# Converting float64 weights with one ScalarE Prelu and two DVE operations, with the prologue and the first batch's runs in a new order

## Chip, cores and metric

One Trainium2 chip, one of its cores. The metric is the device time of one launch in microseconds; the kernel before takes 1564.34 us, the median of three runs (1562.92 to 1564.81). Engines by the profile's names: PE multiplies matrices, ACT applies functions, DVE and POOL do elementwise work, SP issues every DMA.

## The reference

Eight batches, 8 heads, 576 rows, head dimension 64: first 32 packed queries p attend to k and v, then q attends to the packed result, which serves as keys and as values. The output, 4608 tokens of 512 numbers, passes two MLPs of width 2048:

```
pp  = softmax(p k^T / 8) v;   x = softmax(q pp^T / 8) pp
x   = elu(x @ w_in1) @ w_out1
out = (P(h) / (Q(h) + 1e-6)) @ w_out2,  h = x @ w_in2
P(h) = a0 + a1 h + a2 h^2 + a3 h^3;  Q(h) = 1 + |b0||h| + |b1| h^2
```

The four weight matrices arrive as float64, everything else as float32.

## The kernel before

**Precision and tiling.** Each float32 product of the MLPs runs as three matmuls on a split into hi and lo parts (hi hi, hi lo, lo hi). In the first phase a batch's 576 columns form two halves of 288, and a batch is 32 steps (half n, block f of 128 of the 2048 hidden rows). Step s has `a_h` (L316, 6 matmuls into h), `a_act1` (L325, L326: Exp, then Relu), `a_dve1` (L331: g), `a_hi` (L336, ACT's cast ghi), `a_lo` (L341, DVE's glo) and `a_o` (L351, 12 matmuls into four accumulators acc). A run of steps that add into the accumulators ends with `a_evac`; in the first batch a half takes two runs, and the first run's sum is kept in a tile (xpart) and added at the end. The second phase (from some 770 us) runs the second MLP on blocks of 512 tokens; nothing of it is touched.

**The weights.** w_in is cut into four column blocks c of four pieces (i, c, kt), w_out into 16 pieces (o, f); each piece is 128x512. Since s = A pp and x w_in = A (pp w_in), `m_pe` (L276) multiplies a column block with the batch's packed result once it is there, and `m_hi`, `m_lo` (L286, L290) split it: steps with f in column block c need m of c. A piece is loaded raw (two words a number) and converted by `c0` (scaling of the upper words by 2^-112, on ACT or POOL, and where needed a Sign on ACT), `c1` (bit operations on DVE: L431 AND, L433 shift, L438 shift-OR, L441 OR of the lower words' bits) and `c2` (POOL multiplies by the sign). For w_out `c3` (ACT, L501) and `c4` (POOL, L505) split into hi and lo. `w2_up`, `w2_bits`, `w2_hi`, `w2_lo` do this for the second MLP's 32 pieces, six in a batch, from the second batch on, and spill them to DRAM.

**Order.** All engines' queues are written out by hand, in program order. The prologue does the first batch's attention, the first column block's conversion and warm matmuls without use. Then a loop over s from -2 runs, in this order: loads due (`ldq`), `a_h(s+2)`, PE extras (`peq`), `a_hi(s+1)`, `a_act1(s+2)`, `c1` of the pieces due at s with `a_lo(s+1)` between its parts, `a_dve1(s+2)`, other elementwise work (`ewq`), `a_o(s)`. Tuples give the steps: WO and WI for `c1` of the pieces (`c0` a step earlier, `c3` and `c4` one and two later), MS for m of column blocks 1 to 3, SCH for the next batch's attention. Raw pieces pass through buffers whose own weights come later; a buffer that `c1` sets free is loaded again at once (`loads`, `loaded`, on SP's queue in this order). Before, the buffers of k and v hold four raws as well (`spare_open`).

Of the kernel before, what the change touches and what calls it, by code (L numbers as in the profile page):

```python
# [17 lines left out]
# A float32 product runs as three float32r passes (hi*hi + hi*lo + lo*hi) over  # L18
# exact splits x = hi + lo, hi = x rounded to float32r, lo = x - hi.
# [3 lines left out]
def packed_attention_moe_moe2_kernel(  # L23
    ctx: ExitStack,
    tc: tile.TileContext,
    qT: bass.AP,     # [B, 128=(r d), 4, S]   head = 2 j + r
    kT: bass.AP,     # [B, 128=(r d), 4, S]
    v: bass.AP,      # [B, S, H*D]
    pT: bass.AP,     # [B, 128=(r d), 4, 32]
    w_in1: bass.AP,  # [512, 2048] of 32-bit words, or of pairs of them  # L30
    w_out1: bass.AP, # [2048, 512]
    w_in2: bass.AP,  # [512, 2048]
    w_out2: bass.AP, # [2048, 512]
    a2: bass.AP,     # [128, 4]
    b2: bass.AP,     # [128, 2]
    out: bass.AP,    # [4608, 512]
# [320 lines left out]
    def a_evac(s):  # L357
        # whether a sum is complete
# [34 lines left out]
    # piece: ("i", c, kt) or ("o", f), of the first or the second MLP  # L393
# [25 lines left out]
    def w_e(eng, e, raw):  # L419
        hi = words(raw)[1]  # L420
        if eng is nc.scalar:
            eng.activation(e, hi, AF.Copy, scale=2.0 ** -112)
        else:
            eng.tensor_scalar(e, hi, 2.0 ** -112, 0.0, ALU.mult, ALU.add)

    def w_bits(ws, mid=None):
        # (float32 to fill, scaled upper words, raw, room for the signs if taken)
        ws = [(w.bitcast(U32), e.bitcast(U32), *words(raw), sg) for w, e, raw, sg in ws]
        for w, e, lo, hi, sg in ws:
            if sg is not None:  # L430
                nc.vector.tensor_scalar(sg.bitcast(U32), hi.bitcast(U32), 0x80000000, None, ALU.bitwise_and)  # L431
            else:
                nc.vector.tensor_scalar(e, e, 3, None, ALU.logical_shift_left)  # L433
        if mid:
            mid()
        for w, e, lo, hi, sg in ws:
            if sg is not None:
                nc.vector.scalar_tensor_tensor(  # L438
                    e, e, 3, sg.bitcast(U32), ALU.logical_shift_left, ALU.bitwise_or)
        for w, e, lo, hi, sg in ws:  # L440
# [20 lines left out]
    def c0(p, eng, signed):  # L461
        cw[p] = d = dict(raw=raws.pop((0, p)), e=scr.pop(0))
        if F64:
            w_e(eng, d["e"][1], d["raw"])
            if not signed:
                d["sg"] = scr.pop(0)
                nc.scalar.activation(d["sg"][1], words(d["raw"])[1], AF.Sign)

    def c1(ps, mid=None):
        ys = []  # L470
        for p in ps:
# [6 lines left out]
            ys.append(None if "sg" in d else scr.pop(0))  # L478
        if F64:
            w_bits([(cw[p]["w"], cw[p]["e"][1], cw[p]["raw"], y and y[1]) for p, y in zip(ps, ys)], mid)  # L480
# [5 lines left out]
        for p, y in zip(ps, ys):  # L486
            if y:
                scr_free(y)
# [19 lines left out]
    # the second MLP's: on the way, to DRAM as hi and lo  # L508
    w2t = {}

    def w2_up(piece):
        e = T.tile([128, 512], F32, tag="cvt", name=f"cvt{piece}", bufs=2)
        w2t[piece] = [raws.pop((1, piece)), e]
        if F64:
            w_e(nc.gpsimd, e, w2t[piece][0])

    def w2_bits(piece):
        w = T.tile([128, 512], F32, tag="w", name=f"w{piece}")
        raw, e = w2t[piece]
        if F64:  # L520
            w_bits([(w, e, raw, w)])
# [124 lines left out]
    # =====================================================================  # L646
    with tc.manual_schedule():
# [12 lines left out]
        signed = {p: p[0] == "o" and p[1] not in UNS for p in seq}  # L660
        at_seq = {p: i for i, p in enumerate(seq)}
        slot = {}
        spare = []
        count = [0]

        def loads(n=len(seq)):
            for _ in range(n):
# [8 lines left out]
                elif spare:  # L676
                    slot[i] = (None, spare.pop(0))
                    t = slot[i][1]
# [8 lines left out]
        def spare_open(tag):  # L687
            t = P.tile([128, 2, RW], RDT, tag=tag, name=f"raw_{tag}")
            spare.extend(t[:, i, :] for i in range(2))

# [5 lines left out]
        loads(PL[0])  # L696
# [16 lines left out]
        # keeps the tensor engine's clock up while the first loads arrive  # L713
# [16 lines left out]
        i0, i1 = io[:2]  # L730
        G = nc.gpsimd
# [6 lines left out]
        spare_open("k")  # L738
        loads(EX)
        c0(i0[0], G, False)  # L740
        for r in range(2):
            s1_max(0, r)
            s1_exp(0, r, ("E", "A")[r])
            if r == 0:
                c0(i0[1], G, False)
        c1([i0[0]])
        c2(i0[0])
# [6 lines left out]
        t1_ew(0, 0, engs=(A, A))  # L754
        t1_ew(0, 1, "A", engs=(A, A))
        c1([i0[1]])
        c2(i0[1])
        pp_pe(0, 0, extra("ppx0"))
        pp_pe(0, 1, extra("ppx1"))
        spare_open("v")  # L760
        loads(EX)
        c0(i0[2], A, False)
        c0(i0[3], A, False)
# [4 lines left out]
        warm(WARM[4])  # L768
        c1([i0[2]])
        c2(i0[2])  # L770
        c1([i0[3]])
        c2(i0[3])
        s2_pe(0, 0)
        warm(WARM[5])
        c0(oo[0], A, True)
        s2_max(0, 0)
        s2_sub(0, 0, V)
        m_pe(0, 0, extra("mx"))
        if EARLY:
# [29 lines left out]
        def seq_at(s, a, *fns):  # L809
            # fns a step apart; a pair goes to both queues of its step  # L810
# [18 lines left out]
        def consts():  # L829
            # -a0..-a3, unused, |b1|, Ln bias, Exp bias  # L830
# [189 lines left out]
```

## Time and profile before

| | us |
|---|---|
| median of three runs | 1564.34 |
| span of the profiled execution | 1561.9 |
| busy PE, DVE, ACT, POOL | 1521.0, 1140.2, 1025.3, 424.4 |

The profile gives the profiled execution's span, from the first to the last instruction; no separate time of that execution is given, and the runs lie 1.0 to 2.9 us above the span. A row of the order of time tells start, length, engine, line, operation, out<-in, and in brackets the idle time before it and what ended that. A matmul row's length is modelled. In the windows the clock is the granted share of PE's 2.4 GHz.

### The profile page before, as it was taken

The page shows a single profiled execution, that of the slowest core. Times are in us where ns is not written, and L with a number is a line of the kernel's source. Part 1 is how long each engine was busy: PE and PEld are TensorE (multiplying, and loading weights), DVE is VectorE, ACT ScalarE, POOL GpSimd, SP SyncE. Part 2 cuts the span into 40 slices and gives each one's busy share as a digit, 9 for nine tenths or more (in the row PEclk, how much of TensorE's full clock was granted, in tenths as well). Part 3 has the DMA queues.
Part 4 walks back from the last instruction along what each step waited for, and adds up shares of the span by engine and source line. Part 5 has one row for each costly group of instructions (what it writes and reads, how often), then busy time and mean ns, then how long its engine had stood idle before and what let it go on. Part 6 is the DMA issues. An engine that isn't in the chain of part 4 may idle for free.

```text
span 1561.9 us, 25689 instructions
## 1 busy us (share of the span) xinstructions
PE 1521.0 (97%) x9890; PEld 1314.1 (84%) x9890; DVE 1140.2 (73%) x1857; ACT 1025.3 (66%) x1903; POOL 424.4 (27%) x329
## 2 busy tenths in 40 slices
PE   6799999999999999999999999999999999999999
PEld 5678989889898988999988888888888888888887
DVE  5997686776768677554497777778687777778786
ACT  4576566565656656565586777767677767767675
POOL 3664241322214132210122222222222222222221
PEclk8899999999999999999999999999999999999999
DMA  9343443533344353103930202020010202020000
GB/s 347 128 143 108 159 144 116 174 114 126 119 159 144 115 174 109 65 1 141 381 109 1 82 0 81 1 81 1 19 64 1 81 1 81 1 81 0 28 0 28
DMA packets 64172, 144.80 MB, mean 93 GB/s; under 512 B 4784, under 2 KB 24496, under 8 KB 61232
## 3 DMA queue, kind: packets, MB, share of 16 engines
q1 hardware_dynamic: 64048, 143.15, 25.9%
q8 instruction: 77, 1.26, 0.3%
q14 instruction: 47, 0.39, 0.1%
HBM read 98.04 MB, written 45.09 MB: 92 GB/s over the span
## 4 chain that ended last, share of the span: by engine, by line
PE 83%; DVE 11%; ACT 3%; issue 2%; DMA 1%; SPq 0%; POOL 0%; ACTq 0%; DVEq 0%; POOLq 0%
PE accb L631 25%; PE hb L578 25%; PE acc L351 20%; PE h L316 9%; DVE glo L341 1%; DVE g L331 1%; PE m L276 1%; DVE m L290 1%; DVE s2m L245 1%; DMA raw0('i', 0, 3)_97<-in_w_in_dram 1%; ACT e L326 1%; PE s L129 1%; ACT e L325 1%; PE pp L179 1%; DVE s2m L244 1%
## 5 line engine op out<-in xcount | busy, mean ns | idle before, releaser
L351 PE MATMUL acc<-ghi,wo 128*128 128x288 f32 x2048 | 461.2, 301 | 3.3 <-POOL wo L505 2.7
L578 PE MATMUL hb<-xb,w 128*128 128x512 f32 x1728 | 414.6, 389 | 0.0
L351 PEld LDWEIGHTS acc<-ghi,wo 128*128 128x128 f32 x2048 | 343.4, 189 | 46.2 <-ACT e L325 21.3
L578 PEld LDWEIGHTS hb<-xb,w 128*128 128x128 f32 x1728 | 324.4, 188 | 67.3
L631 PE MATMUL accb<-wo,ghi 128*128 128x512 f32 x1152 | 354.6, 389 | 0.0
L623 POOL TENSOR_TENSOR glo<-g,ghi 128x512 fp32r<-128x512 f32 x143 | 185.6, 1298 | 586.9 <-ACT ghi L621 583.8
L351 PE MATMUL acc<-glo,wo 128*128 128x288 f32 x1024 | 304.7, 298 | 11.3 <-DVE glo L341 11.0
L316 PE MATMUL h<-A,m 128*128 128x288 f32 x1536 | 248.4, 297 | 12.6 <-ACT A L262 3.8
L631 PEld LDWEIGHTS accb<-wo,ghi 128*128 128x128 f32 x1152 | 216.2, 188 | 44.7
L341 DVE TENSOR_TENSOR glo<-g,ghi 128x288 fp32r<-128x288 f32 x256 | 162.0, 633 | 106.7 <-ACT ghi L336 106.1
L316 PEld LDWEIGHTS h<-A,m 128*128 128x128 f32 x1536 | 219.4, 190 | 14.4 <-DVE m L290 4.2
L631 PE MATMUL accb<-wo,glo 128*128 128x512 f32 x576 | 224.1, 389 | 0.0
L336 ACT CAST ghi<-g 128x288 fp32r<-128x288 f32 x256 | 110.6, 432 | 151.4 <-PE acc L351 85.6
L351 PEld LDWEIGHTS acc<-glo,wo 128*128 128x128 f32 x1024 | 193.2, 189 | 15.8 <-DVE glo L341 15.7
L331 DVE SCALAR_TENSOR_TENSOR g<-e,h 128x288 f32<-128x288 f32 x256 | 115.3, 450 | 96.2 <-ACT e L326 95.6
L612 DVE SCALAR_TENSOR_TENSOR Q<-Q,L 128x512 f32<-128x512 f32 x144 | 99.8, 693 | 103.0 <-ACT L L606 103.0
L592 ACT ACTIVATE w<-hb,ab_sb 128x512 f32<-128x512 f32 x144 | 98.5, 684 | 88.5 <-PE hb L578 88.5
L621 ACT CAST ghi<-g 128x512 fp32r<-128x512 f32 x144 | 89.7, 623 | 95.8 <-PE accb L631 61.1
L325 ACT ACTIVATE e<-h 128x288 f32<-128x288 f32 x256 | 105.1, 411 | 63.7 <-PE h L316 62.6
L631 PEld LDWEIGHTS accb<-wo,glo 128*128 128x128 f32 x576 | 108.2, 188 | 22.6 <-DVE glo L623 0.2
L615 DVE SCALAR_TENSOR_TENSOR g<-t,cf,Q 128x512 f32<-128x512 f32 x144 | 108.3, 752 | 16.6 <-DVE Q L613 0.5
L326 ACT ACTIVATE e<-e 128x288 f32<-128x288 f32 x256 | 113.9, 445 | 8.1
(412 smaller groups left out, 1696.8 us busy)
## 6 DMA issues: line engine op xcount, KB each, us to landing
xb<-x2d SPq DMA_DIRECT2D x18, 1024.0 KB, 7.3
x2d<-x SPq DMA_DIRECT2D x30, 576.0 KB, 3.4
out_dram<-o SPq DMA_DIRECT2D x35, 256.0 KB, 2.1
v<-in_v_dram SPq DMA_DIRECT2D x8, 1024.0 KB, 6.3
w<-wi2d SPq DMA_DIRECT2D x8, 1024.0 KB, 10.8
wo<-wo2d SPq DMA_DIRECT2D x16, 512.0 KB, 11.4
k<-in_kT_dram SPq DMA_DIRECT2D x7, 1152.0 KB, 6.5
q<-in_qT_dram SPq DMA_DIRECT2D x7, 1152.0 KB, 5.2
```

What stands on the lines that cost most here:

```text
L316: nc.tensor.matmul(ps[:, :TA], lhsT=m[:, wx, r, c0:c0 + 128], rhs=A[:, ax, r, :], start=(i == 0), stop=(i == 5))
L325: nc.scalar.activation(d["e"], d["h"][:, :TA], AF.Exp)
L326: nc.scalar.activation(d["e"], d["e"], AF.Relu, scale=-1.0, bias=1.0)
L331: nc.vector.scalar_tensor_tensor(d["g"], d["e"], -1.0, d["h"][:, :TA], ALU.mult, ALU.max)
L336: nc.scalar.copy(d["ghi"], d["g"])
L341: nc.vector.tensor_tensor(d["glo"], d["g"], d["ghi"].bitcast(F32), ALU.subtract)
L351: nc.tensor.matmul(acc[m][:, :TA], lhsT=w[:, wx, m * 128:(m + 1) * 128], rhs=d[g], start=(first and i == 0), stop=(last and i == 2))
L578: nc.tensor.matmul(ps, lhsT=w[:, k, c0:c0 + 128], rhs=x[:, k, :], start=(i == 0), stop=(i == 3 * NKD - 1))
L612: nc.vector.scalar_tensor_tensor(Q, Q, 1.0 + 1e-6, r, ALU.add, ALU.mult)
L615: nc.vector.scalar_tensor_tensor(d["g"], t, cf[:, 0:1], Q, ALU.add, ALU.mult)
L623: eng.tensor_tensor(d["glo"], d["g"], d["ghi"].bitcast(F32), ALU.subtract)
L631: nc.tensor.matmul(acc[m], lhsT=d[g][:, m * 128:(m + 1) * 128], rhs=w[:, wx, :], start=(f == 0 and i == 0), stop=(f == NF - 1 and i == 2))
```

## The change

One Prelu on ACT gives a non-negative float for either sign: scale 2^-112 as before, and for negative numbers a slope of -2^32, which adds 32 to the exponent, so that the shift by three moves a bit into the sign's place. Sign, AND, shift-OR and POOL's multiply are gone, in both MLPs. The first batch's runs are four steps of half 0, eight of half 1, twelve of half 0, eight of half 1. Pieces, m and loads have new steps; only the first column block is converted, and o0 scaled, ahead of the loop. Scratch is one pair in wo15 and four tiles; k's and v's buffers hold no raws. The diff, cut:

```diff
-    EARLY = 1
-    S2 = -2
-    MS = (1, 11, 17)
+    RUNS = (0, 0, 4), (1, 0, 8), (0, 4, 16), (1, 8, 16)
+    MS = (5, 13, 17)
-    UNS = (3, 7, 8, 9, 11, 12, 14)
-    EA = (1, 2, 3, 8, 12)
-    WO = (-2, -1, 0, 0, 1, 2, 3, 4, 13, 13, 15, 16, 17, 18, 19, 21)
-    WI = (-2, -2, -1, -1, 5, 6, 8, 7, 10, 11, 11, 12)
+    WO = (-2, -1, 0, 1, 5, 6, 7, 8, 12, 13, 14, 15, 16, 17, 18, 19)
+    WI = (1, 2, 3, 4, 8, 9, 10, 11, 12, 13, 14, 15)
-    NWS = NF - 3
-    PL, EX = (2, 2, 6), 2
+    NWS = NF - 1
...
-            g, i = divmod(t, NF // 2)
-            return b, g % 2, i + NF // 2 * (g // 2), (i == 0, i == NF // 2 - 1)
+            for n, f0, f1 in RUNS:
+                if t < f1 - f0:
+                    return b, n, f0 + t, (t == 0, t == f1 - f0 - 1)
+                t -= f1 - f0
...
+    def w_e(e, raw):
+        nc.scalar.activation(e, words(raw)[1], AF.Prelu, scale=2.0 ** -112, alpha=-2.0 ** 32)
     def w_bits(ws, mid=None):
+        ws = [(w.bitcast(U32), e.bitcast(U32), words(raw)[0]) for w, e, raw in ws]
+        for w, e, lo in ws:
+            nc.vector.tensor_scalar(e, e, 3, None, ALU.logical_shift_left)
         if mid:
             mid()
+        for w, e, lo in ws:
             nc.vector.scalar_tensor_tensor(w, lo, 29, e, ALU.logical_shift_right, ALU.bitwise_or)
...
-    def c2(p):
-        d = cw[p]
-        if "sg" in d:
-            nc.gpsimd.tensor_tensor(d["w"], d["w"], d["sg"][1], ALU.mult)
-            scr_free(d["sg"])
...
         load_k(0, HALVES)
-        loads(PL[0])
+        loads(1)
         load_v(0)
         lq = load_q(0, HALVES)
         next(lq)
-        loads(PL[1])
+        loads(3)
         next(lq)
-        loads(PL[2])
+        loads(1)
         nc.sync.dma_start(out=ab_sb[:, 0:4], in_=a2)
         nc.sync.dma_start(out=ab_sb[:, 4:6], in_=b2)
+        loads()
...
+        t1_ew(0, 0, engs=(A, V))
+        t1_ew(0, 1, "A", engs=(A, V))
+        c0(i0[0])
         pp_pe(0, 0, extra("ppx0"))
         pp_pe(0, 1, extra("ppx1"))
+        c1([i0[0]])
         pp_ew(0, 0)
         pp_ew(0, 1)
         ppt_pe(0, extra("pptx"))
         ppt_ew(0)
         warm(WARM[4])
+        s2_pe(0, 0)
+        c0(i0[1])
+        warm(WARM[5])
+        s2_max(0, 0)
+        c1([i0[1]])
+        c0(i0[2])
+        s2_sub(0, 0, V)
+        s2_exp(0, 0)
         c1([i0[2]])
+        c0(i0[3])
         s2_sum(0, 0)
         s2_mul(0, 0, V)
+        c1([i0[3]])
+        m_pe(0, 0, extra("mx"))
+        s2_pe(0, 1, extra("s2x"))
+        c0(oo[0])
         s2_tr(0, 0)
         s2_hi(0, 0)
+        m_hi(0, 0, slice(0, 256))
+        s2_lo(0, 0, V)
+        m_lo(0, 0, slice(0, 256))
+        s2_max(0, 1, "E")
+        s2_sub(0, 1)
+        m_hi(0, 0, slice(256, 512))
         m_lo(0, 0, slice(256, 512))
+        s2_exp(0, 1)
+        s2_sum(0, 1)
+        warm(WARM[6])
...
-        at(ldq, 13, scr_close, "wo")
-        at(ldq, 14, scr_k)
+        at(ldq, 19, scr_close, "wo")
...
-            seq_at(S2, (0, 1), s2_sum, s2_mul, s2_tr, s2_hi, s2_lo)
+        seq_at(-2, (0, 1), s2_mul, s2_tr, s2_hi, s2_lo)
```

## Rows read from the trace of the kernel before

**Rows 1.** Page, busy us of each engine (share of the span) xinstructions.
```profile
PE 1521.0 (97%) x9890; PEld 1314.1 (84%) x9890; DVE 1140.2 (73%) x1857; ACT 1025.3 (66%) x1903; POOL 424.4 (27%) x329
```

**Rows 2.** Windows: from:to length, busy us by engine (xinstructions), clock, DMA share, GB/s.
```profile
34.00:62.00 28.00, 16.70 (x81) 13.36 (x80) 26.36 (x38) 12.35 (x26) 18.43 (x14) 0.65 0.41 147
62.00:109.00 47.00, 42.51 (x409) 37.32 (x407) 43.06 (x76) 37.90 (x84) 30.47 (x25) 1.00 0.44 155
109.00:140.00 31.00, 28.77 (x257) 23.62 (x250) 27.41 (x50) 19.42 (x41) 19.18 (x15) 1.00 0.18 64
```

**Rows 3.** Timeline of PE, 31 to 63 us: start, us, what, [idle before <-releaser].
```profile
31.82 0.40 PE L316 MATMUL h<-A,m 128*128 128x288 f32 x1 [3.77 <-ACT A L262]
...
41.89 0.61 PE L351 MATMUL acc<-glo,wo 128*128 128x288 f32 x1 [3.00 <-DVE glo L341]
...
62.07 0.30 PE L351 MATMUL acc<-ghi,wo 128*128 128x288 f32 x1
```

**Rows 4.** Chain of waits, first 160 us: start, us, what (one step of PE).
```profile
97.58 0.79 PE h L316 x6
98.38 1.60 PE acc L351 x12
```

**Rows 5.** Timeline of DVE and POOL, 33 to 42 us.
```profile
33.15 0.42 DVE L433 TENSOR_SCALAR scr_cvt<-scr_cvt 128x512 uint32<-128x512 uint32 x1
...
34.20 0.69 DVE L441 SCALAR_TENSOR_TENSOR scr_wo<-raw0('o', 0)_100,scr_wo 128x512 uint32<-128x512 uint32 x1
...
36.02 0.45 DVE L331 SCALAR_TENSOR_TENSOR g<-e,h 128x288 f32<-128x288 f32 x1
...
38.44 1.34 POOL L250 TENSOR_TENSOR s2x<-s2x,s2m 128x576 f32<-128x576 f32 x1
38.69 1.37 DVE L433 TENSOR_SCALAR scr_whi<-scr_whi 128x512 uint32<-128x512 uint32 x1
...
41.38 0.45 DVE L341 TENSOR_TENSOR glo<-g,ghi 128x288 fp32r<-128x288 f32 x1
```

**Rows 6.** DMA issues of the first 60 us: issue, count, KB each, us to landing.
```profile
raw0('i', 0, 3)_97<-in_w_in_dram SPq DMA_DIRECT2D x1, 512.0 KB, 13.6
...
raw0('i', 2, 2)_414<-in_w_in_dram SPq DMA_DIRECT2D x1, 512.0 KB, 3.9
```

**Rows 7.** Timeline of ACT at 20 us.
```profile
20.53 0.68 ACT L422 ACTIVATE scr_wo<-raw0('i', 0, 3)_97 128x512 f32<-128x512 f32 x1 [1.27 <-DMA raw0('i', 0, 3)_97<-in_w_in_dram]
```

**Rows 8.** Groups of ACT, 32 to 104 us: busy us, mean ns | idle before.
```profile
L326 ACT ACTIVATE e<-e 128x288 f32<-128x288 f32 x18 | 8.0, 445 | 0.6
L336 ACT CAST ghi<-g 128x288 fp32r<-128x288 f32 x18 | 7.7, 430 | 12.9 <-DVE g L331 11.0 <-PE acc L351 1.0 <-DVE sm L151 0.9
L325 ACT ACTIVATE e<-h 128x288 f32<-128x288 f32 x18 | 7.4, 410 | 4.1 <-PE h L316 4.0
L501 ACT CAST wo<-scr_wo 128x512 fp32r<-128x512 f32 x6 | 3.6, 604 | 0.0
```

**Rows 9.** Waits, 135 to 770 us: us in total, times, longest us.
```profile
PE acc L351 <- DVE glo L341: 8.0, 12, 1.2
```

**Rows 10.** Timeline, 197 to 214 us (the second batch).
```profile
197.87 0.40 PE L351 MATMUL acc<-glo,wo 128*128 128x288 f32 x1 [0.32 <-DVE glo L341]
...
206.66 0.43 ACT L336 CAST ghi<-g 128x288 fp32r<-128x288 f32 x1 [2.62 <-DVE g L331]
...
210.60 0.69 DVE L438 SCALAR_TENSOR_TENSOR cvt('i', 0, 3)_2445<-cvt('i', 0, 3)_2445,w('i', 0, 3)_2491 128x512 uint32<-128x512 uint32 x1
210.67 1.92 POOL L267 TENSOR_TENSOR A<-s2y,A 128x576 fp32r<-128x576 f32 x1 [2.56 <-ACT A L262]
...
211.33 1.81 DVE L441 SCALAR_TENSOR_TENSOR w('i', 0, 3)_2491<-raw1('i', 0, 3)_2277,cvt('i', 0, 3)_2445 128x512 uint32<-128x512 uint32 x1
...
213.56 0.40 PE L351 MATMUL acc<-glo,wo 128*128 128x288 f32 x1 [1.16 <-DVE glo L341]
```

**Rows 11.** Timeline of ACT at the start.
```profile
0.74 1.28 ACT L648 ACT_TABLE_LOAD   x1 [0.74 <-PEq L1008]
```

More of the change, by code (lines that the diff above doesn't have):

```diff
@@ L412, in words @@
         return two[:, :, 0], two[:, :, 1].bitcast(F32)
[L419 to L424, printed above, removed]
-    def w_bits(ws, mid=None):
[L428 to L433, printed above, removed]
+    def w_e(e, raw):
+        nc.scalar.activation(e, words(raw)[1], AF.Prelu, scale=2.0 ** -112, alpha=-2.0 ** 32)
+    def w_bits(ws, mid=None):
+        ws = [(w.bitcast(U32), e.bitcast(U32), words(raw)[0]) for w, e, raw in ws]
+        for w, e, lo in ws:
+            nc.vector.tensor_scalar(e, e, 3, None, ALU.logical_shift_left)
         if mid:
             mid()
[L436 to L440, printed above, removed]
+        for w, e, lo in ws:
             nc.vector.scalar_tensor_tensor(w, lo, 29, e, ALU.logical_shift_right, ALU.bitwise_or)
@@ L459, in packed_attention_moe_moe2_kernel, with c0 @@
     cw = {}
-    def c0(p, eng, signed):
+    def c0(p):
         cw[p] = d = dict(raw=raws.pop((0, p)), e=scr.pop(0))
         if F64:
[L464 to L467, printed above, removed]
+            w_e(d["e"][1], d["raw"])
     def c1(ps, mid=None):
-        ys = []
         for p in ps:
@@ L477, in c1 @@
                 d["w"] = wi[p[1]][:, p[2], :]
-            ys.append(None if "sg" in d else scr.pop(0))
         if F64:
-            w_bits([(cw[p]["w"], cw[p]["e"][1], cw[p]["raw"], y and y[1]) for p, y in zip(ps, ys)], mid)
+            w_bits([(cw[p]["w"], cw[p]["e"][1], cw[p]["raw"]) for p in ps], mid)
         else:
@@ L485, in c1 @@
                 mid()
-        for p, y in zip(ps, ys):
-            if y:
-                scr_free(y)
+        for p in ps:
             if p[0] == "i":
@@ L514, in w2_up @@
         if F64:
-            w_e(nc.gpsimd, e, w2t[piece][0])
+            w_e(e, w2t[piece][0])
     def w2_bits(piece):
@@ L520, in w2_bits @@
         if F64:
-            w_bits([(w, e, raw, w)])
+            w_bits([(w, e, raw)])
         else:
@@ L659, in packed_attention_moe_moe2_kernel @@
         seq = sorted(when, key=lambda p: when[p])
-        signed = {p: p[0] == "o" and p[1] not in UNS for p in seq}
         at_seq = {p: i for i, p in enumerate(seq)}
         slot = {}
-        spare = []
         count = [0]
@@ L675, in loads @@
                     slot[i] = (fs[0], None)
-                elif spare:
-                    slot[i] = (None, spare.pop(0))
-                    t = slot[i][1]
                 elif used.count("t") < 2:
@@ L685, in loads @@
                 count[0] += 1
-        def spare_open(tag):
-            t = P.tile([128, 2, RW], RDT, tag=tag, name=f"raw_{tag}")
-            spare.extend(t[:, i, :] for i in range(2))
         def loaded(p):
@@ L729, in packed_attention_moe_moe2_kernel @@
             scr_open("wo", [t[:, i, :] for i in range(2)])
-        i0, i1 = io[:2]
-        G = nc.gpsimd
+        i0 = io[0]
         at_new(0)
@@ L737, in packed_attention_moe_moe2_kernel @@
         warm(WARM[1])
-        spare_open("k")
-        loads(EX)
-        c0(i0[0], G, False)
         for r in range(2):
@@ L743, in packed_attention_moe_moe2_kernel @@
             s1_exp(0, r, ("E", "A")[r])
[L744 to L747, printed above, removed]
         t1_pe(0, 0, extra("t1x"))
@@ L753, in packed_attention_moe_moe2_kernel @@
         s1_inv(0, 1)
[L754 to L757, printed above, removed]
+        t1_ew(0, 0, engs=(A, V))
+        t1_ew(0, 1, "A", engs=(A, V))
+        c0(i0[0])
         pp_pe(0, 0, extra("ppx0"))
         pp_pe(0, 1, extra("ppx1"))
[L760 to L763, printed above, removed]
+        c1([i0[0]])
         pp_ew(0, 0)
@@ L837, in packed_attention_moe_moe2_kernel @@
         at(ewq, 24, consts)
-        def scr_k():
-            sk = P.tile([128, 4, 512], F32, tag="k", name="scr_k")
-            scr_open("k", [sk[:, i, :] for i in range(4)])
         for p in seq[NKD:]:
@@ L846, in packed_attention_moe_moe2_kernel @@
             if p not in cw:
-                at(ewq, max(-2, t - 1), c0, p, A if p[0] == "i" or p[1] in EA else G, signed[p])
+                at(ewq, max(-2, t - 1), c0, p)
             cvq.setdefault(t, []).append(p)
-            fns = ([] if signed[p] else [c2]) + ([c3, c4] if p[0] == "o" else [])
-            for k, fn in enumerate(fns):
-                at(ewq, t + 1 + k, fn, p)
-        at(ldq, 13, scr_close, "wo")
-        at(ldq, 14, scr_k)
+            if p[0] == "o":
+                at(ewq, t + 1, c3, p)
+                at(ewq, t + 2, c4, p)
+        at(ldq, 19, scr_close, "wo")
         for c in range(1, NC):
@@ L856, in packed_attention_moe_moe2_kernel @@
                 at(q, MS[c - 1], fn, 0, c)
-        if EARLY:
-            seq_at(S2, (0, 1), s2_sum, s2_mul, s2_tr, s2_hi, s2_lo)
-        else:
-            s2_at(-2, 0, 1)
+        seq_at(-2, (0, 1), s2_mul, s2_tr, s2_hi, s2_lo)
         at(ldq, LK, load_k, 1)
```

25 lines of the change are left out of this document (removed).

## The prediction

> **What bounds the kernel now.** I read the page's busy shares first, then windows over the start, then PE's own order of time there, and only then the engines that feed it. PE is busy 97% of the span [rows 1], so at most 40.9 us (1561.9 - 1521.0) are idle time, plus what PE loses at a lower clock. The windows show where: from 34 to 62 us PE is busy 16.70 of 28 us at a mean granted clock of 0.65, while DVE is busy 26.36; from 62 to 109 PE is busy 42.51 of 47 at full clock, from 109 to 140 it is 28.77 of 31 [rows 2]. So the first steps of the first batch are bound by DVE, the rest of that batch nearly by PE. PE's order of time says the same step by step: the first h starts at 31.82, the second matmul of the first acc step waits 3.00 us for DVE's glo until 41.89, and the fourth acc step starts only at 62.07 [rows 3]; at full clock a step is 0.79 for h and 1.60 for acc, 2.39 us [rows 4]. Between 36.02, when DVE makes the first g, and 62.07 lie 26.05 us for three and a bit steps.
>
> Why DVE is late is in its own rows. A shift takes 0.42 us and an OR 0.69 when alone; a shift that begins while POOL is in a tensor_tensor (38.44 to 39.78) takes 1.37, and the glo that PE waits for comes only at 41.38, behind such shifts [rows 5].
>
> **The conversion.** Before, a weight piece with its sign taken along costs DVE an AND (like the shift, 0.42), a shift-OR (0.69) and an OR (0.69); one without costs DVE shift and OR (1.11), ACT a Sign and POOL a multiply of some 1.3, as its other tensor_tensors [rows 5, 10]. Of the 32 pieces of the first MLP 9 are of the first kind, 23 of the second; half of the upper-word scalings run on POOL. After, every piece is one ACT Prelu, one shift and one OR. DVE saves 9 x 0.69 = 6.2 us. ACT goes from 39 Sign and Copy passes to 32 Prelu passes; I price a Prelu like the Copy on the same strided words, 0.68 [rows 7]. No row shows a Prelu: from below the exp step's 0.41, from above a pass and one table load, 0.68 + 1.28 (rival three). POOL loses 23 multiplies and 16 scalings. What POOL loses matters through DVE: each POOL operation can hold up a DVE one by about its length.
>
> The stretching is told by the Trainium skill too ("SBUF — State Buffer", section "SBUF: two separate sides"): GpSimd and a DVE instruction that needs the shared port pair exclude one another, and the first to start keeps it to its end. The trace agrees: the shift-OR that began 0.07 us ahead of POOL's subtraction took 0.69, the OR behind it 1.81 [rows 10].
>
> **The first three steps.** Between 34 and 62 us DVE now has, at unstretched durations: six conversions (o1, o2, o3, and three of the second column block) x (0.42 + 0.69) = 6.7, four steps of g and glo x 0.90 = 3.6, a last transpose under 1: 11.2 us against 26.36 [rows 2, 5]. POOL still does the low parts of o0 to o2 and two operations of the attention there; five operations that hold DVE up by half a microsecond each make it 13.7. ACT has per step Exp 0.41, Relu 0.45 and the cast 0.43, plus a Prelu and the cast of a wo 0.60 [rows 8]: 2.6 us, 3.9 in the step with two Prelus and the A cast, 12 to 13 us in all. So 13.5 us stand where 26.05 stood: 12.5 saved. Bounds: 16 us at most saved (PE's four steps of 2.39 at full clock [rows 4] stay), 7 if every POOL operation stretches DVE as the 1.37 and 1.81 rows do and ACT's order adds waits.
>
> **The prologue.** SP now issues i0's first piece, v, a half of q, three more pieces, the other half, o0, a and b, then twelve pieces in a row. The bytes ahead of i0's last piece are the same, so it lands when it did, 13.6 us after its issue, where ACT takes it up at 20.53 [rows 6, 7]; v has one piece of 0.5 MB fewer ahead of it, 1 to 2 us (an estimate: ten half megabytes had landed by 20.5), so the pp products can start earlier. The sign multiply (1.3) leaves the chain to m. Against that DVE, in order, now converts three pieces inside the chain max, subtract, exp, sum, multiply (3.3 us, of which 1.1 lie beside the exp), and the first Exp of the MLP stands on ACT behind the second half's s2_exp, which waits for POOL's subtraction. I take 1.5 us earlier for the first g; bounds -2.2 (two conversions in the chain with nothing won) and +4.
>
> **The order of runs.** Four steps of half 0, then eight of half 1, instead of eight and eight: the second column block, which had to be there at step 4, is due at step 8, so its four pieces leave the prologue, and A of half 1 is due at step 4 instead of 8, which the s2 pieces just reach. The same products are formed and the same number of partial sums stored; the store after step 3 costs 4 copies as that after step 7 did. k's and v's buffers no longer hold raw weights, so SP's load of the next k isn't held behind them. The price: with one step between, some late raws are issued when a slot falls free and read by ACT a step later (i3's last at 13 to 14, o15 at 17 to 18). A lone load takes 3.9 us [rows 6], a step 2.4 to 4: ACT may stand 1 to 2 us at each, with its casts queued behind it.
>
> **The rest of the first batch.** From 62 to 109 PE needs 42.5 and one m product more that was earlier before; ACT was busy 37.90 [rows 2], loses some 4 passes of 0.68, gains 4 casts of 0.60 and the m cast, 1.2 as two of them [rows 8]: 38.8. But steps 12 to 15 carry two conversions each, on ACT 1.29 + 1.36 + 0.60 = 3.2 us a step, with the m cast 4.4. At most 4 us can be won; lost, four steps of 0.9 and the m cast, 5: I take 1.0 won here and 0.5 of the 2.2 idle us up to 140.
>
> **Batches two on.** The second MLP's 32 pieces each lose the AND and the shift-OR for a shift, DVE 0.69 less, and the scaling moves from POOL to ACT. PE waits 8.0 us for glo in 12 places there, at most 1.2 [rows 9]: in each of five batches one like the 1.16 of 213.56 [rows 10] and one of 0.32. The long ones stand behind AND, shift-OR and an OR that POOL's subtraction (from 210.67) stretched to 1.81 [rows 10]. With the shift at the AND's place the OR starts near 210.5, ahead of POOL, and glo can start near 211.2, a stretched OR earlier; the short ones need 0.32 of 0.69. ACT's added pass falls in that batch in the 2.62 us in which ACT waits for g [rows 10]. I take 6 us of 7.5; bounds 0 (POOL wins the start) and 7.5. By the skill's rule above the five long waits go if the OR starts first, 5.8 us, and stay if POOL does.
>
> **Sum.** Saved 12.5 + 1.5 + 1.0 + 0.5 + 6.0 = 21.5 us: span 1561.9 - 21.5 = 1540.4. The runs' median, 1564.34, lies 2.4 above this profile's span, so the time is about 1543.
>
> **Rivals.**
> 1. *ACT is the new bound.* Every scaling now sits in ACT's queue ahead of casts that PE needs, and late raws stop it. For it: 38.8 of 47 us and the clumped steps; against: the Signs go. The first steps then save 8 and the stretch to 140 loses 4, with 5 in the later batches: 1564.3 - 9 - 1.5 = about 1554.
> 2. *PE bound from the first step.* The lower clock of 0.65 came with PE's idle stretches [rows 2]; if they go at once, the first steps save 16, the prologue 3, the rest of the batch 5, and later batches 7.5: 1533.
> 3. *The Prelu changes the table.* The trace has one table load in all, 1.28 us at 0.74 [rows 11], and Exp, Relu, Sign and Copy run under it; nothing in it shows Prelu. If Prelu is not in that set, each of 64 needs a load and the next Exp another, 2.57 us: 27 in the first batch's steps where ACT is full, 69 us, and 32 later, each 2.57 less the 1.1 us that ACT is idle in a step (2.39 - 1.29 [rows 4, 8]), 47; less the prologue's and DVE's gain of 21: about 1660. It ends slower than now from the ninth such pair on ACT's critical steps (21.5 / 2.57). The Trainium skill ("ScalarE: Activation LUTs", section "Table sets: the hidden batching unit") says that cheap functions are in every set and names relu, copy, identity and abs, not Prelu; no run here shows it.
> 4. *The second part of the gain doesn't come.* The added ACT pass makes ghi late in later batches as often as DVE's relief makes glo early: 1549.
>
> **Chances.** Forecast 0.58 (its own range 1536 to 1550), rival one 0.15, two 0.10, three 0.06, four 0.11. The 1533 of rival two and the 1554 of rival one set the range: 1533 to 1555. A measurement of this kernel tells about 0.2% (3.1 us) from no change. Faster: all but rival three and the bad end of rival one, 0.89; same 0.03; slower 0.08.
>
> **What would show it.** In the profile after: the first g at 34 to 35, the fourth acc step at 46 to 50 instead of 62.07, DVE's shifts mostly 0.42, POOL far below its 18.43 of 28 us in the first steps; the waits of PE for glo after 140 us down to 1 or 2 us; a Prelu near 0.68 and one table load. Wrong it would be if ACT's cast is what PE waits for in steps 11 to 18, if the first h starts later than 31.82, or if more table loads stand in ACT's rows.

## The result, and the profile after

The changed kernel takes 1545.41 us (median of four runs, 1544.90 to 1547.23), against 1564.55 us for the kernel before (median of four): a ratio of 0.9879, 95% interval 0.9865 to 0.9893. It is 1.2% faster. The forecast was 1543.0 with a range of 1533 to 1555, so size and side were right; the sum behind it was not right in every term, and one half of the change, the new order, turned out to cost time.

The page of the profile after (span 1543.9 us), the line that answers to [rows 1]:

```profile
PE 1516.7 (98%) x9890; PEld 1311.7 (85%) x9890; DVE 1099.6 (71%) x1818; ACT 1038.8 (67%) x1926; POOL 352.9 (23%) x258
```

DVE lost 41 us and POOL 72, ACT gained 13.5; the span lost 18.0. The windows of [rows 2] in the kernel after:

```profile
34.00:62.00 28.00, 25.16 (x175) 22.15 (x176) 24.97 (x46) 21.79 (x48) 8.65 (x7) 0.88 0.54 187
62.00:109.00 47.00, 38.60 (x368) 33.42 (x366) 36.81 (x75) 31.77 (x69) 12.30 (x10) 0.93 0.45 152
109.00:140.00 31.00, 31.00 (x276) 26.64 (x274) 22.82 (x45) 20.30 (x44) 11.69 (x8) 1.00 0.32 114
```

The first window is the gain: PE is busy 25.16 of 28 us in place of 16.70, at a clock of 0.88 in place of 0.65. The second is the surprise: PE is busy 3.9 us less than before there, at a clock of 0.93 in place of 1.00. PE's timeline, the answer to [rows 3] (first h, first glo product, fourth acc step):

```profile
30.58 1.83 PE L316 MATMUL h<-A,m 128*128 128x288 f32 x12
...
37.41 0.44 PE L351 MATMUL acc<-glo,wo 128*128 128x288 f32 x1
...
47.65 0.29 PE L351 MATMUL acc<-ghi,wo 128*128 128x288 f32 x1
```

The wait of 3.00 us for the first glo is gone and the fourth acc step starts 14.4 us earlier. What becomes of that lead is read at a marker that every version has once in five steps, ACT's cast of a second-MLP weight. ACT's timeline before, and then after:

```profile
167.81 0.62 ACT L528 CAST whi('i', 0, 0)_1945<-w('i', 0, 0)_1913 128x512 fp32r<-128x512 f32 x1 [0.45 <-DVE w('i', 0, 0)_1913 L441]
...
638.28 0.60 ACT L528 CAST whi('o', 15)_8128<-w('o', 15)_8096 128x512 fp32r<-128x512 f32 x1
```

```profile
157.80 0.60 ACT L504 CAST whi('i', 0, 0)_1888<-w('i', 0, 0)_1857 128x512 fp32r<-128x512 f32 x1
...
620.21 0.61 ACT L504 CAST whi('o', 15)_8040<-w('o', 15)_8009 128x512 fp32r<-128x512 f32 x1
```

So the lead is 14.4 us at the fourth step, only 10.0 at the first piece of the second MLP (167.81 - 157.80) and 18.1 at the last (638.28 - 620.21). In the kernel before the first of these casts waits 0.45 us for the old conversion of its own piece, which belongs to the later batches; without that the lead there is 9.6. So 4.9 us are lost in the rest of the first batch, and 8.5 are won in the five later ones. Of the 4.9 some 1.1 us are work put off: the kernel before has formed m of column block 1 by its fourth step, the changed one forms it behind its fifth, and at the seventh, where both have it, the lead is 13.3 (71.50 before, 58.19 after).

The largest loss in this stretch is at one place. Three windows, and then the timeline of all engines in the second of them:

```profile
70.00:80.00 10.00, 9.61 (x110) 8.29 (x110) 8.66 (x20) 6.72 (x17) 0.54 (x1) 1.00 0.20 75
80.00:90.00 10.00, 5.41 (x35) 4.47 (x36) 4.91 (x12) 5.00 (x11) 1.47 (x1) 0.66 0.44 152
85.68:89.70 4.02, 4.02 (x18) 3.98 (x19) 1.12 (x5) 0.58 (x1) 0.00 (x0) 0.50 0.28 106
```

```profile
80.77 1.09 PE L274 MATMUL m<-wi,ppT 64*32 64x512 f32 x16 [0.83 <-ACT E L143]
...
83.38 0.98 ACT L284 CAST m<-m 128x1024 fp32r<-128x1024 f32 x1
84.40 1.22 DVE L288 TENSOR_TENSOR m<-m,m 128x1024 fp32r<-128x1024 f32 x1 [1.28 <-ACT m L284]
...
85.68 1.11 PE L157 MATMUL t<-ident,E 128*128 128x128 f32 x4 [3.81 <-DVE sm L149]
...
86.66 0.59 PE L351 MATMUL acc<-ghi,wo 128*128 128x288 f32 x1
...
89.69 1.15 PE L316 MATMUL h<-A,m 128*128 128x288 f32 x6
```

At step 13 PE forms m of column block 2, then has the transposition of the second head half's scores next in its order, and stands 3.81 us. The page names DVE's sm (a 0.14 us operation), but sm stands in DVE's queue right behind the low part of m at 84.40, which is the operation that ended. PE's next h needs m only a step later. But the transposition and m use the same PSUM buffer (the pool "misc" has one), so the transposition waits until m's high part (ACT) and low part (DVE) are read out, and the accumulations of step 13 stand behind it in PE's order. The granted clock averages 1.00 from 70 to 80 us, 0.66 from 80 to 90 and 0.50 from 85.68 to 89.70: after the pause PE runs at the lower of its two levels, 1.2 in place of 2.4 GHz, where the transposition takes 1.11 in place of 0.60 us (e1 below) and the step's accumulations, 86.66 to 89.69, take 3.03 in place of 1.60 [rows 4].

### The profile page after: what moved, and what is told of

Its sections match the earlier page's. It is cut to its first block, busy times and chain, and to the rows that moved or that the text cites. A ratio compares the mean times of both kernels' runs of the same rounds, so it can differ in the third digit from the quotient of the medians.

```text
span 1543.9 us, 25589 instructions
## 1 busy us (share of the span) xinstructions
PE 1516.7 (98%) x9890; PEld 1311.7 (85%) x9890; DVE 1099.6 (71%) x1818; ACT 1038.8 (67%) x1926; POOL 352.9 (23%) x258
## 4 chain that ended last, share of the span: by engine, by line
PE 90%; DVE 5%; ACT 2%; issue 1%; DMA 1%; POOL 0%; SPq 0%; ACTq 0%; POOLq 0%; DVEq 0%
PE accb L607 25%; PE hb L554 25%; PE acc L351 23%; PE h L316 11%; PE m L274 2%; DMA v<-in_v_dram 1%; DVE glo L341 1%; PE s L127 1%; DVE s2m L243 1%; DVE m L288 1%; PE pp L177 1%; ACT e L325 1%; ACT e L326 1%; DVE g L331 0%; PE s L210 0%
## 5 line engine op out<-in xcount | busy, mean ns | idle before, releaser
L591 DVE SCALAR_TENSOR_TENSOR g<-t,cf,Q 128x512 f32<-128x512 f32 x144 | 108.3, 752 | 16.6 <-DVE Q L589 0.5
```

The costliest lines, as they stand in the source:

```text
L591: nc.vector.scalar_tensor_tensor(d["g"], t, cf[:, 0:1], Q, ALU.add, ALU.mult)
```

## The experiments

Two questions: what made the pause at step 13, and which half of the change, the conversion or the new order, won the time. Three chips were used, on which the kernel before takes 1563.61 us (e1, e2, e4, e7), 1564.21 (e5, e6, e8, e10) and 1565.06 (e12 to e15). Each ratio is to the kernel before on the same chip; a difference of medians between chips is known to 1 or 2 us only.

**e1: the transposition one step later.**

```diff
-    SCH = ((6, 8, 10), (12, 13, 15)), (18, 24), (20, 22, 26, 30)
+    SCH = ((6, 8, 10), (12, 14, 15)), (18, 24), (20, 22, 26, 30)
```

> The changed kernel with the scores' transposition of the second head half put at step 14 in place of 13 (SCH's second tuple 12, 14, 15), nothing else. Theory (one PSUM buffer): at step 13 the product m of block 2 and this transposition share the single misc buffer in PSUM; PE issues the transposition and has to wait for m's split on ACT and DVE, 3.8 us, and the accumulations behind it in PE's queue stand as well; the clock falls in the pause. Apart, the wait of 3.81 us in front of the transposition goes, the granted clock between 80 and 90 us stays above 0.9, and the whole gets 4 to 7 us shorter than the changed kernel (about 1540, range 1538.5 to 1541.5). Rival (load of step 13: two conversions, the split of m and the softmax's work are too much for ACT and DVE wherever they are put): the wait moves to the next instruction of PE that needs DVE, and the time stays within 1.5 us of the changed kernel's 1545.4.

Measured 1540.97 us (ratio to before 0.9854, 0.9841 to 0.9868): 4.4 us less than the changed kernel. The window 80 to 90 us in e1, and then the waits around step 14 and the marker:

```profile
80.00:90.00 10.00, 7.84 (x97) 6.21 (x97) 7.12 (x17) 8.03 (x19) 2.78 (x2) 1.00 0.57 200
```

```profile
83.76 0.53 PE L316 MATMUL h<-A,m 128*128 128x288 f32 x2 [0.78 <-ACT m L284]
85.02 0.80 PE L316 MATMUL h<-A,m 128*128 128x288 f32 x4 [0.72 <-DVE sm L149]
85.66 0.60 PE L157 MATMUL t<-ident,E 128*128 128x128 f32 x4
...
152.73 0.60 ACT L504 CAST whi('i', 0, 0)_1888<-w('i', 0, 0)_1857 128x512 fp32r<-128x512 f32 x1
```

The 3.81 us became 0.78 and 0.72, for m itself, which h of step 16 needs, and the clock stays at 1.00. The pause's 3.81, the slow transposition's 0.5 and the slow accumulations' 1.4, less the 1.5 that e1 still waits, are 4.2 us, and 4.4 were measured; in the traces the marker comes 5.1 us earlier (152.73 for 157.80).

**e7: the load of step 13 halved, the collision kept.**

```diff
-    WO = (-2, -1, 0, 1, 5, 6, 7, 8, 12, 13, 14, 15, 16, 17, 18, 19)
+    WO = (-2, -1, 0, 1, 5, 6, 7, 8, 14, 15, 16, 17, 18, 19, 20, 21)
```

> The changed kernel with the conversions of w_out pieces 8 to 15 two steps later (steps 14 to 21 in place of 12 to 19), so that steps 12 and 13 convert one piece each and not two; the product m and the transposition stay at step 13 together. Theory (one PSUM buffer): the pause only loses the part of m's split that stands behind the second Prelu and the second pair of bit operations on ACT and DVE, some 1 to 1.5 us of the 3.81 us, and the time changes by less than 2.5 us (1543 to 1546). Rival (load of step 13): the pause goes, and the time falls by 4 to 7 us to about 1540.

Measured 1545.99 us (0.9879, 0.9863 to 0.9894): no change. Of PE's waits from 62 to 125 us in e7, the two longest:

```profile
PE t L157 <- DVE sm L149: 3.3, 1, 3.3
PE acc L351 <- POOL wo L481: 1.4, 1, 1.4
```

With one conversion in the step the wait is 3.3 in place of 3.8 us, so that half of the load of ACT and DVE makes 0.5 us of the pause and is not its cause. The unchanged time says less: e7 also has a wait of 1.4 us for a wo from POOL, which the changed kernel does not have in this stretch.

**e12: the collision put into the old order** (e6 below, with m of block 2 moved from step 11 to 13).

```diff
-    MS = (1, 11, 17)
+    MS = (1, 13, 17)
```

> The kernel of e6 (old order, new conversion: 1539.2 us) with the product m of block 2 at step 13 in place of 11, where it meets the transposition of the second head half, as in the changed kernel. If the one PSUM buffer that the two share at step 13 is what the new order loses most by, the loss can be put into the old order: PE waits over 3 us for that transposition around 76 to 85 us, the granted clock falls behind it, and the time rises by 3.5 to 6 us, to 1543 to 1545. Rival (the collision costs only beside the new order's conversions at steps 12 and 13): it rises by less than 1.5 us.

Measured 1543.24 us (0.9858, 0.9845 to 0.9871), 4.05 above e6 by medians from two chips; by the ratios it is 2.5 us, and their intervals overlap. Its timeline at step 13, and its marker:

```profile
81.41 1.01 ACT L286 CAST m<-m 128x1024 fp32r<-128x1024 f32 x1
82.45 1.23 DVE L290 TENSOR_TENSOR m<-m,m 128x1024 fp32r<-128x1024 f32 x1 [0.22 <-ACT m L286]
...
83.73 1.11 PE L159 MATMUL t<-ident,E 128*128 128x128 f32 x4 [2.43 <-DVE sm L151]
...
155.50 0.61 ACT L521 CAST whi('i', 0, 0)_1889<-w('i', 0, 0)_1858 128x512 fp32r<-128x512 f32 x1
```

Here the wait is 2.43 us, less than the 3 expected. The traces place the cost: e12 is 0.45 us behind e6 at the fourth acc step (49.91 for 49.46) and 4.3 at the marker (155.50 for 151.18, below), so the collision costs 3.9. Taking it out gained 4.4 by medians and 5.1 by the marker: both sides point to this buffer. A second buffer, which would take away the sharing alone, was not tried.

**e6: the new conversion in the old order.** Everything of the kernel before is kept (prologue, runs, steps, loads) but the conversion, in both MLPs.

```diff
-        hi = words(raw)[1]
-        if eng is nc.scalar:
-            eng.activation(e, hi, AF.Copy, scale=2.0 ** -112)
-        else:
-            eng.tensor_scalar(e, hi, 2.0 ** -112, 0.0, ALU.mult, ALU.add)
+        nc.scalar.activation(e, words(raw)[1], AF.Prelu, scale=2.0 ** -112, alpha=-2.0 ** 32)
...
-            if not signed:
-                d["sg"] = scr.pop(0)
-                nc.scalar.activation(d["sg"][1], words(d["raw"])[1], AF.Sign)
...
-            ys.append(None if "sg" in d else scr.pop(0))
+            ys.append(None)
...
-            w_bits([(w, e, raw, w)])
+            w_bits([(w, e, raw, None)])
```

> The kernel before with its own order of the prologue, its own runs of the first batch, steps of conversion and loads, and only the conversion changed: Prelu on ACT and two bit operations for every piece, no Sign, no product with the sign on POOL. Theory of the prediction (in the first steps the conversion's chain on DVE and POOL is what PE waits for, the order only uses it): 8.5 us from the later batches and 6 to 9 us of the first batch's 9.5 come without the new order: 1546 to 1550. Rival (the new runs ask for fewer converted pieces before the first steps, and that is the gain of the first batch): the later batches' 8.5 us and at most 3 more, 1552 to 1555.

Measured 1539.19 us (0.9842, 0.9828 to 0.9855): below both theories, and 6.2 us less than the changed kernel. PE's fourth acc step and the marker of above in e6:

```profile
49.46 0.30 PE L351 MATMUL acc<-ghi,wo 128*128 128x288 f32 x1
...
151.18 0.61 ACT L521 CAST whi('i', 0, 0)_1889<-w('i', 0, 0)_1858 128x512 fp32r<-128x512 f32 x1
...
613.59 0.61 ACT L521 CAST whi('o', 15)_8041<-w('o', 15)_8010 128x512 fp32r<-128x512 f32 x1
```

It is 16.6 us ahead of the kernel before at the first piece (16.2 without the cast's wait of 0.45 there), 24.7 at the last. The conversion is worth all of the gain and more; the new order costs 6.2. At the fourth acc step the new order is 1.8 us ahead (47.65 for 49.46), and so it is at the seventh (58.19 for 59.96), but at the marker it is 6.6 behind. Of these 8.4 us the buffer makes 5.1 (e1's marker); for the other 3.3, PE's waits from 62 to 125 us sum to 4.9 in e1 (v 1.0, m and its two parts 3.3, aT 0.6) against 2.1 in e6, 2.8 more.

**e4, e5: the second MLP's conversion alone.** e4 has there the three bit operations and POOL's scaling of before; e5 the three operations, but the scaling as a Copy on ACT. The first MLP is as changed.

```diff
-            w_e(e, w2t[piece][0])
+            nc.gpsimd.tensor_scalar(e, words(w2t[piece][0])[1], 2.0 ** -112, 0.0, ALU.mult, ALU.add)
...
-            w_bits([(w, e, raw)])
+            e_, w_ = e.bitcast(U32), w.bitcast(U32)
+            lo_, hi_ = words(raw)
+            nc.vector.tensor_scalar(w_, hi_.bitcast(U32), 0x80000000, None, ALU.bitwise_and)
+            nc.vector.scalar_tensor_tensor(e_, e_, 3, w_, ALU.logical_shift_left, ALU.bitwise_or)
+            nc.vector.scalar_tensor_tensor(w_, lo_, 29, e_, ALU.logical_shift_right, ALU.bitwise_or)
```

e5 has the same three operations, and this in place of the first edit:

```diff
-            w_e(e, w2t[piece][0])
+            nc.scalar.activation(e, words(w2t[piece][0])[1], AF.Copy, scale=2.0 ** -112)
```

> The changed kernel with the second MLP's weights converted as before the change (POOL scales, DVE masks the sign, shifts and ORs it, ORs the low word: three bit operations), the first MLP's and the whole prologue as changed. By the traces the h of each later batch gained 1.72 us in each of five batches, 8.6 us: the time should rise by 8 to 9 us to 1553.5 to 1554.5 if all of that gain comes from this conversion. Rival: part of it comes from elsewhere (the other first-batch layout leaves the later batches' loads at another place), then it rises by 6 us or less, to at most 1551.5.

> The changed kernel with the second MLP's weights scaled on ACT by a plain Copy, and then the three bit operations on DVE as before the change (mask of the sign, shift with OR, OR of the low word). With POOL's scaling and three operations the kernel took 1553.7 us, with the Prelu and two operations 1545.4. Theory of the prediction (the third operation on DVE in front of glo is what PE waits for): the time stays near 1553, 1551 to 1554. Rival (POOL's scaling of 1.3 us, beside which DVE's operations are stretched, was the cost): the time falls to 1545.5 to 1547.5.

Measured 1553.69 (0.9936, 0.9923 to 0.9948) and 1553.08 us (0.9930, 0.9917 to 0.9942). The waits of PE from 125 to 752 us in e4, in e5 and in the changed kernel (us in total, times, longest):

```profile
PE acc L351 <- DVE glo L341: 8.1, 12, 1.2
```

```profile
PE acc L351 <- DVE glo L341: 7.7, 12, 1.2
```

```profile
PE acc L351 <- DVE glo L341: 3.2, 7, 0.6
```

The old conversion gives 8.3 us back, and taking POOL's scaling out of it changes 0.6, which the intervals don't tell apart: in the later batches the gain is DVE's third operation.

**e14: the old order, the first MLP with ACT's Copy and three operations of DVE**, no Sign, no work of POOL in the conversion, the second MLP with Prelu. Against e6:

```diff
-        nc.scalar.activation(e, words(raw)[1], AF.Prelu, scale=2.0 ** -112, alpha=-2.0 ** 32)
+        if eng is nc.scalar:
+            nc.scalar.activation(e, words(raw)[1], AF.Copy, scale=2.0 ** -112)
+        else:
+            nc.scalar.activation(e, words(raw)[1], AF.Prelu, scale=2.0 ** -112, alpha=-2.0 ** 32)
...
-            w_e(eng, d["e"][1], d["raw"])
+            w_e(nc.scalar, d["e"][1], d["raw"])
...
-            ys.append(None)
+            ys.append(scr.pop(0))
```

> The kernel of e6 with the first MLP's 28 pieces scaled on ACT by a plain Copy and then three bit operations on DVE (mask, shift with OR, OR), the second MLP's by Prelu: no scaling and no sign's product on POOL at all, but 0.69 us more of DVE for a piece. The new conversion gained 16.6 us in the first batch of e6. If that is DVE's saved operation, as it was in the second MLP, most of it goes: 1548 to 1554. If it is POOL's work that went from the chain (scaling 1.3 us, product 1.34 us, and DVE's operations stretched beside them), most of it stays: 1539 to 1543.

Measured 1555.68 us (0.9939, 0.9926 to 0.9951), 16.5 above e6, and 15.4 above e15 (below), which is as fast as e6 and ran on e14's chip. Its marker:

```profile
169.57 0.61 ACT L524 CAST whi('i', 0, 0)_1921<-w('i', 0, 0)_1890 128x512 fp32r<-128x512 f32 x1
```

The number of pieces in the expectation was wrong: all 32 are concerned. 32 x 0.69 = 22.1 us more on DVE cost 15.4 to 16.5, so about 0.7 of every microsecond on DVE is paid here. It leaves the first batch where it was before the change (marker 1.8 us later than before's, 2.2 without the wait of 0.45 there). So in the first batch the old route by Sign and POOL's product was no better than a third operation of DVE, and only a conversion with neither gains.

**e8: POOL's product put back** into the changed kernel, on scratch that nobody reads, for the twelve w_in pieces converted in the steps.

```diff
...
+    def c2(p):
+        e = cw[p]["e"]
+        nc.gpsimd.tensor_tensor(e[1], e[1], e[1], ALU.mult)
+        scr_free(e)
...
+            if p[0] == "i":
+                at(ewq, t + 1, c2, p)
```

> The changed kernel with one more operation on POOL, a product of 128x512 of scratch whose value nothing uses, one step after the conversion of each of the twelve w_in pieces that are converted in the steps of the first batch, like the sign's product of before. Nothing waits for it but the next use of that scratch. Theory (DVE's bit operations and glo are stretched beside POOL's, as 0.68 to 1.37 and 1.81 us in the kernel before): 8 of the 12 fall in steps that PE waits in, at 0.3 to 0.7 us each, and the time rises by 2.5 to 6 us, to 1548 to 1551.5. Rival (POOL is out of the way once the conversions' order is new): within 1 us of 1545.4.

Measured 1547.80 us (0.9901, 0.9887 to 0.9914), 2.4 more: just under the theory's end, above the rival's. The intervals overlap by a little, but the marker too comes 2.5 us later than the changed kernel's:

```profile
160.30 0.60 ACT L509 CAST whi('i', 0, 0)_1900<-w('i', 0, 0)_1869 128x512 fp32r<-128x512 f32 x1
```

DVE is busy 4.9 us longer with the same 1818 instructions (1104.5 for 1099.6), so it is held up beside POOL. The edit also keeps the scratch a step longer, and what part that has is not shown. A product that nobody waits for costs 0.2 us on average.

**e15, e13: more of POOL's work off DVE's way, in the old order.** e15 is e6 with the second half's `s2_mul` of the first batch on DVE; e13 also moves the next batch's first scores from step 6 to 7.

```diff
-            seq_at(S2, (0, 1), s2_sum, s2_mul, s2_tr, s2_hi, s2_lo)
+            seq_at(S2, (0, 1), s2_sum, lambda b, hf: s2_mul(b, hf, V), s2_tr, s2_hi, s2_lo)
```

```diff
-    SCH = ((6, 8, 10), (12, 13, 15)), (18, 24), (20, 22, 26, 30)
+    SCH = ((7, 8, 10), (12, 13, 15)), (18, 24), (20, 22, 26, 30)
```

> The kernel of e6 with one operation moved: the product of the second head half's probabilities with the reciprocal sum (128x576, 1.16 us on POOL at 33.85 us) goes to DVE. In e6 three shifts of DVE took 3.07 us beside it and beside the split of wo on POOL (0.36 to 0.45 each elsewhere), and PE waited 2.16 us for glo behind them. If DVE is held up by POOL's operations, the shifts fall to some 2 us or less in all, the product costs 0.76 us on DVE, and the wait falls by 0.5 to 1.3 us: time 1537.8 to 1538.8. If the shifts are slow for another reason, DVE only has 0.76 us more in front of glo: 1539.5 to 1540.

> The kernel of e15 and beside that the next batch's first scores one step later (step 7 in place of 6), since PE waited 1.36 us there for the transfer of k, which waits for two raw weights' slots. If both waits go: 1536.5 to 1537.8. If the scores' chain then comes late for its transposition at step 8, the wait only moves: as e15 or up to 1 us more.

Measured 1540.29 (0.9841, 0.9827 to 0.9854) and 1539.60 us (0.9836, 0.9823 to 0.9850): as e6. The timeline of POOL and DVE in e6 at 33 us, and then in e15:

```profile
33.85 1.16 POOL L250 TENSOR_TENSOR s2x<-s2x,s2m 128x576 f32<-128x576 f32 x1 [8.15 <-ACT e L326]
34.97 1.44 POOL L498 TENSOR_TENSOR wo<-scr_wo,wo 128x512 fp32r<-128x512 f32 x1
...
33.62 3.07 DVE L429 TENSOR_SCALAR scr_wo<-scr_wo 128x512 uint32<-128x512 uint32 x3
36.61 0.45 DVE L341 TENSOR_TENSOR glo<-g,ghi 128x288 fp32r<-128x288 f32 x1
```

```profile
35.97 1.42 POOL L498 TENSOR_TENSOR wo<-scr_wo,wo 128x512 fp32r<-128x512 f32 x1 [8.54 <-DVE scr_wo L429]
...
35.22 1.03 DVE L429 TENSOR_SCALAR scr_wo<-scr_wo 128x512 uint32<-128x512 uint32 x3
36.16 1.54 DVE L341 TENSOR_TENSOR glo<-g,ghi 128x288 fp32r<-128x288 f32 x1
```

The three shifts fell from 3.07 to 1.03 us, as expected of a hold-up by POOL; but glo, which now begins 0.19 us after POOL's split of wo, took 1.54 in place of 0.45, and the product itself is DVE's now: 2.0 us won, 1.1 and 0.7 lost. PE's first wait for glo fell from 2.16 to 1.20 us, but the two traces start further apart than that (first h at 28.61 and 30.21), so the medians could hardly show it.

**e2, e10: v earlier, and a better place for m.** e2 requests the next batch's v at step 2; e10 has that, and m at step 12, scores at 13, transposition at 14.

```diff
-    LK, LV = (1, 8)
+    LK, LV = (1, 2)
```

```diff
-    MS = (5, 13, 17)
+    MS = (5, 12, 17)
...
-    SCH = ((6, 8, 10), (12, 13, 15)), (18, 24), (20, 22, 26, 30)
+    SCH = ((6, 8, 10), (13, 14, 15)), (18, 24), (20, 22, 26, 30)
```

> The changed kernel with the next batch's v requested at step 2 in place of step 8. Theory: v's transfer landed too late for the first product with it at 70 us (PE waited 1.52 and 0.28 us for it), since its request stood on SP behind raw weights that wait for free slots; earlier it is there in time, and the kernel gets 1 to 2 us shorter (1543.5 to 1544.5). Rival: the transfer then takes the queue from the raw weights, which come later, and PE gets the same wait or more at the weights' conversion: 1545 to 1548.

> A candidate from the first four runs: the changed kernel with the product m of block 2 at step 12 (before: 13), the second head half's scores at 13, their transposition at 14 and product at 15 (before: 12, 13, 15), and the next batch's v requested at step 2. If the one PSUM buffer is what these four wait for, each then has it free when it comes, and the rest of waits at steps 12 to 14 of the kernel with the transposition alone moved (0.86 for the buffer, 0.78 and 0.72 us for m's split) goes as well, with 1 us for v: 1537 to 1539. If the splits of m now stand behind the conversions at step 12, it gains nothing over the transposition alone moved: 1540 to 1541.5.

e2 took 1544.58 us (0.9875, 0.9862 to 0.9889): PE no longer waits for v, but 0.8 us is too little to tell from nothing. e10 took 1540.17 us (0.9847, 0.9833 to 0.9860), no better than e1 within its interval. PE's waits from 62 to 125 us in e10 show why: the one buffer now makes the scores wait for m, and the transposition waits for the scores' exp.

```profile
PE s L127 <- DVE m L288: 1.8, 1, 1.8
PE t L157 <- ACT E L143: 1.7, 1, 1.7
```

No version tried is clear of e6: e13 has a lower ratio, e1 and e10 lie 1.8 and 1.0 us above, and all these intervals overlap with e6's. So of the 6.2 us that the new order costs, the collision's part is shown by e1; what the rest is, only the waits above tell.

## Why the prediction was right, step by step

- *First three steps 12.5 and prologue 1.5: right in size.* The first g in the kernel after:

```profile
34.74 0.44 DVE L331 SCALAR_TENSOR_TENSOR g<-e,h 128x288 f32<-128x288 f32 x1
```

  It came 1.3 us earlier than at 36.02, but in the eight traces with this prologue the first h lies between 29.00 and 30.68, so that this term agrees with the forecast is partly luck. From the first g to the fourth acc step stand 12.9 us for 13.5 forecast. That step came 14.4 us earlier for 14.0 forecast, within the 46 to 50 named. Whose gain it is the prediction left open; e6 shows that 12.6 of it (62.07 - 49.46) come with the conversion in the old order.
- *Rest of the first batch, 1.0 won to 109 us and 0.5 to 140: this term failed*, by 6.4 us: -4.9 in place of +1.5 up to the marker. The loss came within the 5 us that the prediction kept as the bound, but for another reason: it priced the two conversions a step on ACT, and e7 shows that these don't decide. "The m product more that was earlier before" was in the sum as PE's time only; which PSUM buffer it holds at its new step, and who asks for that buffer next, wasn't asked. Without the collision (e1) the marker's lead is 14.6 (15.1 less the wait of 0.45), so this part would have been +0.2; what is still missing to the forecast 1.5 is probably in e1's waits for v and m, but no run separates that.
- *Later batches 6.0 of at most 7.5: the mechanism was right in its first half, and the size was 8.5, above the bound.* As forecast the Prelu (0.67 us) falls into ACT's idle time, the shift stands where the AND stood, and the OR begins ahead of POOL's subtraction. The changed kernel in the second batch, all engines, the answer to [rows 10]:

```profile
193.74 0.67 ACT L420 ACTIVATE cvt('i', 0, 3)_2386<-raw1('i', 0, 3)_2219 128x512 f32<-128x512 f32 x1
...
200.34 0.69 DVE L430 SCALAR_TENSOR_TENSOR w('i', 0, 3)_2432<-raw1('i', 0, 3)_2219,cvt('i', 0, 3)_2386 128x512 uint32<-128x512 uint32 x1
200.43 1.89 POOL L265 TENSOR_TENSOR A<-s2y,A 128x576 fp32r<-128x576 f32 x1 [3.40 <-ACT A L260]
200.95 1.69 DVE L341 TENSOR_TENSOR glo<-g,ghi 128x288 fp32r<-128x288 f32 x1
...
202.69 0.40 PE L351 MATMUL acc<-glo,wo 128*128 128x288 f32 x1 [0.52 <-DVE glo L341]
```

  The OR did start first, but glo itself is now the operation held up (1.69 us), which the prediction left out: the long wait fell from 1.16 to 0.52 and didn't go. By the matmul rows 8.0 - 3.2 = 4.8 us were won. The rest was missed because the bound was read from those rows: their lengths are modelled and cover part of a wait, so that short ones don't show. The weight load in front of a late product waits as well. PEld's waits for glo over these batches, before and then after:

```profile
PEld acc L351 <- DVE glo L341: 12.4, 18, 1.4
```

```profile
PEld acc L351 <- DVE glo L341: 4.9, 8, 0.8
```

  12.4 - 4.9 = 7.5 us. After such a wait the next product starts 0.23 us behind the late one (213.56 and 213.79 before), in place of 0.13 in the flow (209.00 and 209.13); at ten places fewer that is 1.0 us more, an estimate, and with it the 8.5 are there.
- *Sum:* 14.4 - 4.9 + 8.5 = 18.0 us for 21.5 forecast; errors of +0.4, -6.4 and +2.5. That the last two cancel in part is luck, not foresight. The median lies 1.5 us above the profile's span, for 2.4 assumed, so the time came out 2.4 above the forecast and not 3.5.
- *The rivals.* ACT as the bound (1554) had the right steps but not the cause. PE bound from the first step (1533) isn't reached: PE idles, and its clock is 0.88, in the first window. The table: one load stands in the trace after, and the Prelu is as short as the Copy that stood at [rows 7]:

```profile
0.73 1.28 ACT L624 ACT_TABLE_LOAD   x1 [0.73 <-PEq L953]
...
12.30 0.66 ACT L420 ACTIVATE scr_cvt<-raw0('i', 0, 0)_86 128x512 f32<-128x512 f32 x1
```

  That the later gain doesn't come (1549) is refuted by e4. Of the signs named, PE's waits for glo after 140 us were to fall to 1 or 2 us, and 3.2 are left. DVE's shifts were "mostly 0.42" as named, 19 of 28 between 30 and 110 us; the other nine took 0.86 to 1.14, each begun beside a tensor_tensor of POOL.

## What to carry to other kernels

When a product is moved to another step, list who holds its PSUM buffer at that step and who asks for it next: in PE's order one small transposition that waits for a buffer stops the accumulations behind it, and 3.8 us of waiting cost 4.4 (e1). Test the parts of a change apart even when the whole is faster: here the conversion alone was worth 25 us and the new order took 6 back. Read the size of a stall from the weight loads' rows as well as from the matmuls'.

## What the runs showed of the hardware that was not expected

A DVE operation that gets out of POOL's way can leave the hold-up to the next one in DVE's queue. In the later batches the OR now starts ahead of POOL's subtraction and takes 0.69 in place of 1.81 us, and glo behind it takes 1.69; in e15, without POOL's product, the three shifts take 1.03 in place of 3.07, and glo takes 1.54. The Trainium skill ("SBUF — State Buffer", section "SBUF: two separate sides") says that of a DVE and a GpSimd operation which want the shared port pair the one that starts first holds it to its end; the rows agree, with 0.09 us of head start for the OR at 200.34, and 0.19 us of delay for the glo at 36.16.

After the pause of 3.81 us in the changed kernel the granted clock was 0.50 from 85.68 to 89.70 us and averaged 0.66 from 80 to 90; with the pauses of 0.78 and 0.72 of e1 it stayed at 1.00.
